# Turned operands stored token by token, and read with a step, in a recurrence and mixing kernel on one core

## The chip, the cores and the metric

The kernel runs on one core of a Trainium2 chip, with fp32 inputs in HBM and an fp32 output there. The metric is the time of one execution on the device in microseconds (us); less is better. The engines are TensorE (PE, with its weight loads shown apart as PEld), VectorE (DVE), ScalarE (ACT), GpSimd (POOL) and SyncE (SP, which only issues transfers here).

## The reference

Four batches, eight heads, 768 tokens, 40 numbers per head. The first part is a recurrence over tokens with a 40x40 state for each head; its output, with the heads side by side (320 numbers per token), goes through a mixing block.

```python
for t in range(S):
    y[:, :, t] = np.einsum('bhd,bhde->bhe', rt, state)
    Sa = np.einsum('bhde,bhe->bhd', state, at)
    state_decay = state * wt[:, :, None, :] - np.einsum('bhd,bhe->bhde', Sa, bt)
    state = state_decay + np.einsum('bhd,bhe->bhde', vt, kt)

theta = x @ w_theta
zr, zi = x * np.cos(theta), x * np.sin(theta)
y = np.einsum('ts,bsd->btd', w_tok_r, zr) + np.einsum('ts,bsd->btd', w_tok_i, zi)
u = x + y
out = u + np.maximum(u @ w_ch, 0.0)
```

## The kernel before

**Chunks.** The recurrence is computed in chunks of 128 tokens: 6 chunks per batch, 24 in all, numbered i. For each chunk, decays are summed by a product with a triangular matrix, k, b and a are scaled by them, and the scaled operands are turned (transposed on TensorE) so that heads and their 40 numbers lie on partitions. Two heads share a turned block: head 2g on partitions 0 to 39, head 2g+1 on 64 to 103. So there are G = 4 pairs g, and a turned operand of a chunk is a tile of 128 partitions x 512 bf16 numbers. Between tokens of the chunk there are four score matrices (`scores`, lines 530 to 553): `spsi` and `sphi` from kbT and aT, `slv` from vT and rT, `slu` from nuT and rT. Each is eight matmuls of 64x128 by 64x128 (4 pairs x 2 halves of the partitions), all at line 537, into a tile of two PSUM banks, and then a masked copy to SBUF. `recurrence` takes the state on by one chunk, `readout` makes the chunk's output: at line 723 four matmuls of rT against the state of before, with rT as the stationary operand, then for each head one with `lamv` (line 730) and one with `lamu` (line 732).

**How r and v are turned.** r is loaded for two chunks at a time in long runs (line 405): partition p of the loaded tile is 4t + g, t counting groups of eight tokens, and eight tokens q lie along the partition. `turn_runs` (line 500) casts this to bf16 and makes eight transposes (line 509), one for each q, into one PSUM bank; within each the 128 columns are (t, g). Two copies on ScalarE (line 513), one for each of the two chunks, read that bank with a step and write SBUF in the order (g, t, q), so that in rT the 128 tokens of a pair g lie side by side. For chunks 0 to 7 (`RUNS = 8`) v is loaded and turned in the same way (tile names `raw_v`, `o`, `vT`), and `turn_back` (line 519) turns vT again into the form with tokens on partitions; for chunks 8 to 23 v is turned from its own cast by `tr` (line 479), pair by pair. That makes 12 calls of `turn_runs` for r and 4 for v: 128 transposes, and 24 + 8 copies at line 513. In all these transposes the tile that is turned is the stationary operand, and the unit matrix `wide` streams.

**Copies of whole words.** Other turned tiles leave PSUM through `evac` (line 386): ScalarE copies pairs of bf16 numbers as 32-bit words (`copy_words`, line 381), or VectorE copies them as bf16 numbers (`copy_halves`, line 384).

**The order of the work.** The program makes a list of operations; each names its engine, and operations may carry an alternative on another engine. `ORDER` gives the order in which the operations are issued, written out by hand as numbers, `HOMES` the PSUM bank of each result, and `PICK` the operations that take their alternative. The costs that an operation is given (592 for the copies at line 513) are not used after that. Before, the copies at line 513 have no alternative, and no number of theirs stands in `PICK`. Waits between engines follow from who writes and reads what.

Of the kernel before, what the change touches and what calls it, by code (L numbers as in the profile page):

```python
# [10 lines left out]
BF16 = mybir.dt.bfloat16  # L11
# [10 lines left out]
RUNS = 8  # L22
# [178 lines left out]
def mm(n):  # L201
    return max(n / 2.4 + 2.5, 25.0)


def tail(n):
    return 166 + n / 2.4 - mm(n)
# [3 lines left out]
def kernel(  # L210
# [14 lines left out]
    nc = tc.nc  # L225
# [4 lines left out]
    G = H // 2  # L230
# [9 lines left out]
    def sb(name, shape, dt, n):  # L240
        return [consts.tile(shape, dt, name=f"{name}_{i}") for i in range(n)]
# [31 lines left out]
    ident = wide[:, 64:192]  # L273
# [46 lines left out]
    for n, (i, t) in sorted(enumerate(to_zero), key=lambda e: e[1][0]):  # L320
# [12 lines left out]
    nuT_t = sb("nuT", [128, 512], BF16, 2)  # L333
# [18 lines left out]
                i=sb("wtok_i", [128, NT, 128], BF16, NT))  # L352
# [7 lines left out]
    def ps(key):  # L360
        h = plan.home[key]
        return doubles[h[0] // 2] if len(h) == 2 else singles[h[0] - DOUBLE]

    def rows(p):
        return slice(64 * p, 64 * p + 64)

    def add(eng, kind, i, fn, cost, reads=(), writes=(), at="tile", **kw):
        return plan.add(eng, kind, i, fn, cost, tuple(reads), tuple(writes),
                        (at, i, kind), **kw)

    def pair(t, g):
        return t[:, 2 * g:2 * g + 2, :].rearrange("p a b -> p (a b)")

    def transpose_pairs(dst, srcs):
        for j, src in enumerate(srcs):
            for g in range(G):
                c = (j * G + g) * 128
                nc.tensor.transpose(out=dst[:, c:c + 128], in_=pair(src, g), identity=ident)  # L378

    def copy_words(out, in_):  # L380
        nc.scalar.copy(out=out.bitcast(FP32), in_=in_)  # L381

    def copy_halves(out, in_):
        nc.vector.tensor_copy(out=out, in_=in_.bitcast(BF16))
# [25 lines left out]
    def run_key(nm, i, c):  # L410
        return ("raw_v", i % 6 + c) if nm == "o" else ("raw_r", i // 2 % 2, c)
# [7 lines left out]
    def cast(kind, i, dst, src, reads, writes, fast):  # L419
        act = ("ACT", lambda: nc.scalar.copy(out=dst, in_=src))  # L420
        pool = ("POOL", lambda: nc.gpsimd.tensor_copy(out=dst, in_=src))
        one, two = (act, pool) if fast else (pool, act)
        add(one[0], kind, i, one[1], 0, reads, writes, alts=(two,))
# [76 lines left out]
    def turn_runs(nm, i, t, raw, dsts):  # L500
        s = i // 2 % 2
        cast(nm, i, t[:, :, :, 0:D], raw.rearrange("p c (q d) -> p q c d", q=8),
             [run_key(nm, i, 0), run_key(nm, i, 1)], [(nm, s)], i == 0)
        pr = ("ps", "t" + nm, i)

        def go():
            d = ps(pr).bitcast(BF16)
            for q in range(8):
                nc.tensor.transpose(out=d[:, q * 128:q * 128 + 128],  # L509
                                    in_=t[:, q].rearrange("p c d -> p (c d)"), identity=ident)  # L510
        add("PE", "t" + nm, i, go, 8 * mm(128), [(nm, s)], [pr], new=(pr, 1), tail=tail(128))
        for x, (dst, dkey) in enumerate(dsts):
            add("ACT", "e" + nm, i + x, lambda x=x, dst=dst: nc.scalar.copy(  # L513
                out=dst.rearrange("p (g t q) -> p g t q", g=G, q=8),
                in_=ps(pr).bitcast(BF16).rearrange(
                    "p (q t g) -> p g t q", q=8, g=G)[:, :, 16 * x:16 * x + 16]),
                592, [pr], [dkey])

    def turn_back(i):
        p, vT, vb = ("ps", "tb", i), vT_t[i % NTR], v_t[i % NRV]  # L520

        def go():
            d = ps(p).bitcast(BF16)
            for g in range(G):
                nc.tensor.transpose(out=d[:, g * 128:g * 128 + 128],
                                    in_=vT[:, g * 128:g * 128 + 128], identity=ident)
        add("PE", "tb", i, go, 4 * mm(128), [("vT", i % NTR)], [p], new=(p, 1), tail=tail(128))
        evac("ACT", "eb", i, p, vb.rearrange("p h d -> p (h d)"), 512, writes=[("v", i % NRV)])

    def scores(i, kind, kindm, lhs, rhs, keys, dst, dkey, mask):  # L530
        p = ("ps", kind, i)

        def go():
            t = ps(p).rearrange("p a (g c) -> p a g c", g=G)
            for g in range(G):
                for q in range(2):
                    nc.tensor.matmul(t[:, q, g, :],  # L537
                                     lhsT=lhs[rows(q), g * 128:(g + 1) * 128],
                                     rhs=rhs[rows(q), g * 128:(g + 1) * 128],
                                     start=True, stop=True)  # L540
        add("PE", kind, i, go, 8 * 26, keys, [p], new=(p, 2), mode=64, tail=tail(128))
        flat = dst.rearrange("p a b c -> p (a b) c")
        sign = -1.0 if mask is mask_n else 1.0

        def whole():
            return ps(p).rearrange("p a (g c) -> p (a g) c", c=128)
        add("DVE", kindm, i, lambda: nc.vector.tensor_tensor(  # L547
            out=flat, in0=whole(), in1=mask.to_broadcast([128, 2 * G, 128]), op=ALU.mult),
            1217, [p], [dkey], alts=(("ACT", lambda: nc.scalar.mul(
                out=flat, in_=whole(), mul=sign)),))  # L550
        add(None, "sel", i, None, 0, [dkey], [dkey], alts=(("POOL", lambda: nc.gpsimd.affine_select(
            out=flat, in_=flat, pattern=[[0, 2 * G], [1, 128]], compare_op=ALU.is_gt,
            fill=0.0, base=0, channel_multiplier=-1)),))

    def attention_scores(i):
        st, s2 = i % NTR, i % NSC
        kbT, aT, vT, rT = kbT_t[st], aT_t[st], vT_t[st], rT_t[i // 2 % 3][:, i % 2]
        scores(i, "spsi", "mpsi", kbT[:, 0:512], aT, [("kbT", st), ("aT", st)],
               psi_t[s2], ("psi", s2), mask_p)
        scores(i, "sphi", "mphi", kbT[:, 512:], aT, [("kbT", st), ("aT", st)],  # L560
               phi_t[s2], ("phi", s2), mask_n)
        scores(i, "slv", "mlv", vT, rT, [("vT", st), ("rT", i % 6)],
               lamv_t[s2], ("lamv", s2), mask_p)

    def recurrence(i):
# [114 lines left out]
    def x_key(q):  # L680
        return ("xs", q % 2) if alone(q) else ("x", q % NX)
# [27 lines left out]
    def readout(i):  # L709
        first = i % NCH == 0  # L710
        s2 = i % NSC
        rT, kb = rT_t[i // 2 % 3][:, i % 2], kb_t[i % NKB]
        scores(i, "slu", "mlu", nuT_t[i % 2], rT,
               [("nuT", i % 2), ("rT", i % 6)], lamu_t[s2], ("lamu", s2), mask_p)
        lamv, lamu = lamv_t[s2], lamu_t[s2]
        gd = gd_t[(i + 1) % 2]
        pk = ("ps", "y", i)

        def y():
            t = ps(pk)  # L720
            for g in range(G):
                if not first:
                    nc.tensor.matmul(t[:, g * 80:g * 80 + 80],
                                     lhsT=rT[:, g * 128:(g + 1) * 128],
                                     rhs=gd[:, 2 * g:2 * g + 2, :], start=True,
                                     stop=False, skip_group_check=True)
                for p in range(2):
                    h = 2 * g + p
                    o = t[:, h * D:h * D + D]
                    nc.tensor.matmul(o, lhsT=lamv[:, p, g, :], rhs=kb[:, 0, h, 0:D],  # L730
                                     start=first, stop=False, skip_group_check=True)
                    nc.tensor.matmul(o, lhsT=lamu[:, p, g, :], rhs=kb[:, 1, h, 0:D],  # L732
                                     start=False, stop=True, skip_group_check=True)
        add("PE", "y", i, y, 16 * 25 + (0 if first else 4 * mm(80)),
            [("rT", i % 6), ("lamv", s2), ("lamu", s2), ("kb", 0, i % NKB),
             ("kb", 1, i % NKB)] + ([] if first else [("gd", (i + 1) % 2)]), [pk],
            new=(pk, 1), tail=tail(40))
        x = x_of(i)
        add("DVE", "ex", i, lambda: nc.vector.tensor_tensor(
            out=x.rearrange("p (g c d) -> p g c d", c=2, g=G),  # L740
            in0=ps(pk)[:, 0:DM].rearrange("p (g c d) -> p g c d", c=2, g=G),
            in1=we_t[i % NEX].rearrange("p (g c d) -> p g c d", c=2, g=G),
            op=ALU.mult), 488, [pk, ("we", i % NEX)], [x_key(i)])
# [186 lines left out]
    for o in plan.order():  # L930
        if o.idx in WARM:
            t = ps(o.new[0])
            t = t[:, 0] if len(t.shape) == 3 else t
# [39 lines left out]
```

## Time and profile before

| | |
|---|---|
| time, median of 3 runs | 201.24 us (200.72 to 202.55) |
| the profiled execution's own time | 199.71 us |
| its span, first to last instruction | 198.0 us |
| TensorE, VectorE, ScalarE, GpSimd busy | 96%, 85%, 79%, 72% of the span |
| transposes of r and v, line 509 | 96 + 32 |
| score matmuls, line 537 | 384 of kbT and aT, 192 of vT and rT, 192 of nuT and rT |
| matmuls with rT as stationary operand, line 723 | 80 |
| copies of rT and vT, line 513 | 24 of 596 ns, 8 of 590 ns |

A row of a group of instructions reads: line, engine, operation, what is written <- what is read, shapes and number of them | busy time in us, mean ns of one | idle time of the engine just ahead of them, with what ended it. Matmuls run in a pipeline: the time of one includes its way through the array, and the next starts long before it ends, so the distance between starts tells what one costs. PEld rows are weight loads, which run beside the matmuls.

### The profile page before, as it was taken

Reading aid. Unit: us, or ns where it says so; the run is one execution under the profiler, and the core shown is the slowest. Engines: PE = TensorE matmul, PEld = TensorE weight load, DVE = VectorE, ACT = ScalarE, POOL = GpSimd, SP = SyncE. Lnnn points to the kernel's source line nnn. Section 1 sums busy time; section 2 is a strip of 40 time slices with the busy share of each in tenths; the row PEclk is TensorE's granted clock in tenths of the full one; section 3 lists DMA queues with packets and bytes.
Section 4 is the critical chain, followed back from the end, with each engine's and each line's share of the span. In section 5 each row is a group of like instructions: output and inputs, shape, how many; then the busy total and the mean of one; then the engine's idle time right before and its main releaser. Section 6 shows DMA issues by size and latency. Waiting matters only on the chain.

```text
span 198.0 us, 8123 instructions
## 1 busy us (share of the span) xinstructions
PE 189.6 (96%) x3354; PEld 153.8 (78%) x3354; DVE 167.6 (85%) x263; ACT 156.2 (79%) x345; POOL 142.3 (72%) x207
## 2 busy tenths in 40 slices
PE   7888999998999999999999999999999999999992
PEld 6777787876887788877787978887788878777761
DVE  5279899999999898986897999999999986878553
ACT  3687889999999989699986898889998957565110
POOL 8277574689998999799799767888598684319300
PEclk9999999999999999999999999999999999999999
DMA  6999899999999899999989989989947350020213
GB/s 117 220 195 200 147 199 188 201 179 201 184 196 174 161 196 181 225 190 209 185 189 167 205 183 205 175 171 174 195 73 160 74 140 3 33 70 15 89 66 132
DMA packets 127365, 31.03 MB, mean 157 GB/s; under 512 B 117664, under 2 KB 127328, under 8 KB 127328
## 3 DMA queue, kind: packets, MB, share of 16 engines
q1 hardware_dynamic: 124544, 27.54, 69.5%
q0 software_dynamic: 2784, 2.97, 9.7%
q8 instruction: 26, 0.43, 0.9%
q14 instruction: 11, 0.09, 0.1%
HBM read 29.54 MB, written 3.93 MB: 169 GB/s over the span
## 4 chain that ended last, share of the span: by engine, by line
PE 71%; ACT 10%; SPq 6%; DVE 5%; issue 4%; DMA 2%; POOL 0%; DVEq 0%; ACTq 0%
PE ps_s L809 16%; PE ps_s L378 12%; PE ps_d L537 9%; PE ps_s L693 6%; SPq L395 4%; PE ps_s L661 4%; PE ps_s L617 3%; PE ps_s L509 3%; DMA raw_kb<-in_k_dram 2%; PE ps_s L703 2%; PE ps_s L596 2%; SPq L407 2%; PE ps_s L732 2%; PE ps_s L884 2%; PE ps_d L809 2%
## 5 line engine op out<-in xcount | busy, mean ns | idle before, releaser
L415 POOL TENSOR_TENSOR kb<-raw_kb,ex 128x320 bf16<-128x320 f32 x46 | 36.9, 812 | 8.1 <-ACT ex L448 2.7
L809 PE MATMUL ps_s<-zr,wtok_r 128*128 128x320 bf16 x132 | 37.5, 299 | 0.0
L809 PE MATMUL ps_s<-zi,wtok_i 128*128 128x320 bf16 x132 | 37.5, 299 | 0.0
L547 DVE TENSOR_TENSOR lamu<-ps_d,mask_p 128x1024 bf16<-128x1024 f32 x23 | 27.9, 1216 | 0.3 <-PE ps_d L537 0.3
L547 DVE TENSOR_TENSOR psi<-ps_d,mask_p 128x1024 bf16<-128x1024 f32 x22 | 26.8, 1218 | 0.7 <-PE ps_d L537 0.5
L547 DVE TENSOR_TENSOR phi<-ps_d,mask_n 128x1024 bf16<-128x1024 f32 x19 | 23.2, 1219 | 1.4 <-PE ps_d L537 1.4
L793 POOL TENSOR_TENSOR zi<-cs,xp 128x320 bf16<-128x320 f32 x21 | 16.4, 793 | 9.2 <-ACT cs L778 9.2
L547 DVE TENSOR_TENSOR lamv<-ps_d,mask_p 128x1024 bf16<-128x1024 f32 x17 | 20.7, 1219 | 2.6 <-PE ps_d L537 2.4
L415 POOL TENSOR_TENSOR ah<-raw_a,we 128x320 bf16<-128x320 f32 x22 | 19.0, 868 | 4.0 <-ACT we L457 3.0
L793 POOL TENSOR_TENSOR zr<-cs,xp 128x320 bf16<-128x320 f32 x21 | 16.6, 804 | 2.2 <-ACT cs L778 2.2
L809 PEld LDWEIGHTS <-wtok_r 128*128 128x128 bf16 x144 | 14.0, 97 | 4.1
L537 PE MATMUL ps_d<-aT,kbT 64*128 64x128 bf16 x384 | 16.9, 217 | 0.3 <-ACT kbT L381 0.2
L632 POOL TENSOR_TENSOR gt<-sum,ex 128x320 bf16<-128x320 f32 x13 | 9.6, 736 | 10.6 <-DVE sum L628 7.6
L809 PEld LDWEIGHTS <-wtok_i 128*128 128x128 bf16 x144 | 14.0, 97 | 3.4
L378 PE MATMUL ps_s<-wide,kb 128*128 128x128 bf16 x192 | 15.3, 223 | 0.5 <-ACT th L758 0.3
L513 ACT COPY rT<-ps_s 128x512 bf16<-128x512 bf16 x24 | 13.3, 596 | 1.9 <-PE ps_s L509 1.6
L730 PE MATMUL ps_s<-kb,lamv 128*128 128x40 bf16 x192 | 14.7, 180 | 0.0
L732 PE MATMUL ps_s<-kb,lamu 128*128 128x40 bf16 x192 | 14.6, 179 | 0.0
L537 PEld LDWEIGHTS <-kbT 64*128 64x128 bf16 x384 | 11.7, 94 | 3.5 <-ACT kbT L381 1.3
L833 DVE SCALAR_TENSOR_TENSOR oo<-ps_s,up 128x320 f32<-128x320 f32 x21 | 9.5, 486 | 5.1 <-PE ps_s L703 4.2
L730 PEld LDWEIGHTS <-lamv 128*128 128x128 bf16 x192 | 13.2, 96 | 0.5
L378 PEld LDWEIGHTS <-kb 128*128 128x128 bf16 x192 | 12.0, 100 | 1.4 <-POOL kb L415 0.6
(166 smaller groups left out, 615.8 us busy)
## 6 DMA issues: line engine op xcount, KB each, us to landing
raw_w<-in_w_dram SPq DMA_DIRECT2D x24, 160.0 KB, 4.0
raw_v<-in_v_dram SPq DMA_DIRECT2D x24, 160.0 KB, 3.9
raw_a<-in_a_dram SPq DMA_DIRECT2D x24, 160.0 KB, 4.0
raw_kb<-in_k_dram SPq DMA_DIRECT2D x24, 160.0 KB, 3.8
raw_kb<-in_b_dram SPq DMA_DIRECT2D x24, 160.0 KB, 4.2
raw_r<-in_r_dram SPq DMA_DIRECT2D x24, 160.0 KB, 3.7
out_dram<-oo SPq DMA_DIRECT2D x23, 160.0 KB, 2.2
wrow_i<-in_moe_w_tok_i_dram POOLq DMA_DIRECT2D x6, 192.0 KB, 5.1
```

The costliest lines, as they stand in the source:

```text
L378: nc.tensor.transpose(out=dst[:, c:c + 128], in_=pair(src, g), identity=ident)
L415: pool = ("POOL", lambda: nc.gpsimd.tensor_tensor(out=dst, in0=in0, in1=in1, op=ALU.mult))
L513: add("ACT", "e" + nm, i + x, lambda x=x, dst=dst: nc.scalar.copy(out=dst.rearrange("p (g t q) -> p g t q", g=G, q=8), in_=ps(pr).bitcast( ...
L537: nc.tensor.matmul(t[:, q, g, :], lhsT=lhs[rows(q), g * 128:(g + 1) * 128], rhs=rhs[rows(q), g * 128:(g + 1) * 128], start=True, stop=True)
L547: add("DVE", kindm, i, lambda: nc.vector.tensor_tensor(out=flat, in0=whole(), in1=mask.to_broadcast([128, 2 * G, 128]), op=ALU.mult), 1217 ...
L632: add("POOL", "wgt", i, lambda: nc.gpsimd.tensor_tensor(out=new_state, in0=sum_t, in1=wm.to_broadcast([128, 8, D]), op=ALU.mult), 830, [(" ...
L693: nc.tensor.matmul(ps(pk)[:, 0:DM], lhsT=lhs[:, c * n + kt, :], rhs=wt[:, 3 * c + kt, :], start=kt == 0, stop=kt == 2, skip_group_check=n ...
L730: nc.tensor.matmul(o, lhsT=lamv[:, p, g, :], rhs=kb[:, 0, h, 0:D], start=first, stop=False, skip_group_check=True)
L732: nc.tensor.matmul(o, lhsT=lamu[:, p, g, :], rhs=kb[:, 1, h, 0:D], start=False, stop=True, skip_group_check=True)
L793: pool = ("POOL", lambda: nc.gpsimd.tensor_tensor(out=dst, in0=in0, in1=in1, op=ALU.mult))
L809: nc.tensor.matmul(acc(), lhsT=wtok[nm][j][:, s], rhs=zs[c][:, s], start=n == 0 and c == 0, stop=n == NT - 1 and c == 1)
L833: add("DVE", "oo", t, lambda ck=ck, u=u, oo=oo: nc.vector.scalar_tensor_tensor(out=oo, in0=ps(ck)[:, 0:DM], scalar=0.0, in1=u, op0=ALU.max ...
```

## The change

The eight transposes of `turn_runs` write to PSUM with a step: for each token (t, q) its four pairs g lie side by side (8 bytes), and the tokens of the two chunks follow one another. The two halves of the bank are then each the wanted tile in the order (token, g), and ScalarE copies each as 256 32-bit words. The copies are given an alternative on VectorE; `ORDER`, `HOMES` and `PICK` stay as they are. Where rT is read (scores `slv` and `slu`, line 723), and vT of chunks 0 to 7 (`slv`, `turn_back`), a pair's 128 tokens now lie four numbers apart; `by_token` gives these views and `by_pair` the ones with neighbouring tokens, which the other operands keep.

```diff
+    def by_pair(t):
+        return [t[:, g * 128:g * 128 + 128] for g in range(G)]
+
+    def by_token(t):
+        return [t.rearrange("p (t g) -> p g t", g=G)[:, g] for g in range(G)]
...
         def go():
-            d = ps(pr).bitcast(BF16)
+            d = ps(pr).bitcast(BF16).rearrange("p (t q g) -> p q t g", q=8, g=G)
             for q in range(8):
-                nc.tensor.transpose(out=d[:, q * 128:q * 128 + 128],
+                nc.tensor.transpose(out=d[:, q],
                                     in_=t[:, q].rearrange("p c d -> p (c d)"), identity=ident)
...
-            add("ACT", "e" + nm, i + x, lambda x=x, dst=dst: nc.scalar.copy(
-                out=dst.rearrange("p (g t q) -> p g t q", g=G, q=8),
-                in_=ps(pr).bitcast(BF16).rearrange(
-                    "p (q t g) -> p g t q", q=8, g=G)[:, :, 16 * x:16 * x + 16]),
-                592, [pr], [dkey])
+            words = ("ACT", lambda x=x, dst=dst: copy_words(
+                dst, ps(pr)[:, 256 * x:256 * x + 256]))
+            halves = ("DVE", lambda x=x, dst=dst: copy_halves(
+                dst, ps(pr)[:, 256 * x:256 * x + 256]))
+            add("ACT", "e" + nm, i + x, words[1], 512, [pr], [dkey], alts=(halves,))
...
     def turn_back(i):
...
                 nc.tensor.transpose(out=d[:, g * 128:g * 128 + 128],
-                                    in_=vT[:, g * 128:g * 128 + 128], identity=ident)
+                                    in_=by_token(vT)[g], identity=ident)
...
     def scores(i, kind, kindm, lhs, rhs, keys, dst, dkey, mask):
...
                     nc.tensor.matmul(t[:, q, g, :],
-                                     lhsT=lhs[rows(q), g * 128:(g + 1) * 128],
-                                     rhs=rhs[rows(q), g * 128:(g + 1) * 128],
+                                     lhsT=lhs[g][rows(q)], rhs=rhs[g][rows(q)],
                                      start=True, stop=True)
...
-        scores(i, "slv", "mlv", vT, rT, [("vT", st), ("rT", i % 6)],
+        scores(i, "slv", "mlv", (by_token if i < RUNS else by_pair)(vT), by_token(rT),
+               [("vT", st), ("rT", i % 6)],
                lamv_t[s2], ("lamv", s2), mask_p)
...
-        scores(i, "slu", "mlu", nuT_t[i % 2], rT,
+        scores(i, "slu", "mlu", by_pair(nuT_t[i % 2]), by_token(rT),
                [("nuT", i % 2), ("rT", i % 6)], lamu_t[s2], ("lamu", s2), mask_p)
...
                     nc.tensor.matmul(t[:, g * 80:g * 80 + 80],
-                                     lhsT=rT[:, g * 128:(g + 1) * 128],
+                                     lhsT=by_token(rT)[g],
                                      rhs=gd[:, 2 * g:2 * g + 2, :], start=True,
                                      stop=False, skip_group_check=True)
```

The calls of `scores` for `spsi` and `sphi` pass `by_pair` of kbT and aT, which is what was read before.

More of the change, by code (lines that the diff above doesn't have):

```diff
@@ L557, in attention_scores @@
         kbT, aT, vT, rT = kbT_t[st], aT_t[st], vT_t[st], rT_t[i // 2 % 3][:, i % 2]
-        scores(i, "spsi", "mpsi", kbT[:, 0:512], aT, [("kbT", st), ("aT", st)],
+        scores(i, "spsi", "mpsi", by_pair(kbT[:, 0:512]), by_pair(aT), [("kbT", st), ("aT", st)],
                psi_t[s2], ("psi", s2), mask_p)
-        scores(i, "sphi", "mphi", kbT[:, 512:], aT, [("kbT", st), ("aT", st)],
+        scores(i, "sphi", "mphi", by_pair(kbT[:, 512:]), by_pair(aT), [("kbT", st), ("aT", st)],
                phi_t[s2], ("phi", s2), mask_n)
-        scores(i, "slv", "mlv", vT, rT, [("vT", st), ("rT", i % 6)],
+        scores(i, "slv", "mlv", (by_token if i < RUNS else by_pair)(vT), by_token(rT),
+               [("vT", st), ("rT", i % 6)],
                lamv_t[s2], ("lamv", s2), mask_p)
```

## The prediction

> **What bounds the kernel now.** I read the page first, then the busy time by stretch, then the chain of waits, then single groups and the timeline of TensorE and ScalarE.
>
> ```profile
> span 198.0 us, 8123 instructions
> PE 189.6 (96%) x3354; PEld 153.8 (78%) x3354; DVE 167.6 (85%) x263; ACT 156.2 (79%) x345; POOL 142.3 (72%) x207
> PE 71%; ACT 10%; SPq 6%; DVE 5%; issue 4%; DMA 2%; POOL 0%; DVEq 0%; ACTq 0%
> ```
>
> TensorE carries 71% of the chain that ended last, ScalarE 10%. Busy time by stretch (busy us and count for PE, weight loads, DVE, ACT, POOL) says where each of them rules:
>
> ```profile
> 40.00:50.00 10.00, 9.19 (x173) 7.21 (x171) 9.89 (x13) 9.88 (x23) 9.75 (x14) 1.00 1.03 193
> 50.00:66.00 16.00, 15.67 (x332) 13.01 (x331) 15.46 (x22) 15.91 (x34) 14.59 (x21) 1.00 1.04 185
> 66.00:176.00 110.00, 109.68 (x2025) 90.28 (x2024) 97.07 (x144) 92.83 (x207) 86.37 (x116) 1.00 0.81 155
> ```
>
> From 66 to 176 us TensorE is idle for 0.32 us in 110: that stretch is as long as TensorE's own work. From 40 to 66 us ScalarE is busy 25.79 of 26 us and VectorE 25.35, while TensorE stands for 1.14. Before 19 us the chain is SP's queue of loads and then one load of k (13.93 to 18.56 us), which the change doesn't touch.
>
> **The change part by part.** *The 32 copies on ScalarE (24 of r, 8 of v).* They now read 256 words, a form that the trace has on the same engine:
>
> ```profile
> L513 ACT COPY rT<-ps_s 128x512 bf16<-128x512 bf16 x24 | 13.3, 596 | 1.9 <-PE ps_s L509 1.6 <-DVE up L815 0.2
> L381 ACT COPY kbT<-ps_s 128x512 f32<-128x512 f32 x16 | 9.4, 586 | 2.1 <-PE ps_s L378 1.6
> L381 ACT COPY vT<-ps_s 128x256 f32<-128x256 f32 x15 | 5.7, 380 | 0.8 <-PE ps_s L378 0.7
> ```
>
> So 596 - 380 = 0.216 us less for each, 32 x 0.216 = 6.9 us of ScalarE in all. The written order and the list of operations moved to another engine are unchanged, so all 32 stay on ScalarE and nothing passes another queue. No instruction is listed as waiting for a copy of line 513; the gain goes to what stands behind it on ScalarE. Copies outside a stretch in which the chain runs through ScalarE give nothing. The chain in order of time passes these:
>
> ```profile
> 29.54 0.51 ACT vT L513
> 30.40 0.58 ACT vT L513
> ...
> 31.93 0.36 PE ps_s L596 x8
> 42.42 0.02 ACT vT L513
> ...
> 42.90 0.59 ACT vT L513
> ...
> 89.92 0.26 ACT rT L513
> 90.29 0.59 ACT rT L513
> ```
>
> Three pairs, 6 x 0.216 = 1.3 us at most. TensorE's longest waits behind them are 0.5 us for nx at 31.9 us (the two copies before it are worth 0.43), 0.3 for nu near 45.5, and 0.3 for th near 92.8, sum 1.1. Where ScalarE stops being late, the next is close: from 21.3 to 27.5 us and from 57.3 to 62.5 the chain is on VectorE, whose busy share from 40 to 66 us is 97%. I take 1.0 us, with 0.4 (the VectorE chain swallows all but one pair) and 3.0 as ends. The 3.0 is ScalarE setting the pace everywhere from 20 to 66 us, where 12 of the copies lie (12 x 0.216 = 2.6), and the pair near 90 us (0.4).
>
> *Writing the transposes to PSUM in runs of four 2-byte elements (8 bytes) with 64 bytes from run to run: 16 x 8 = 128 transposes.* No matmul of the trace writes that way. The nearest row is ScalarE's copy of line 513 itself, which reads this bank with 256 bytes between neighbours at 596 ns, against 586 for 512 neighbouring words: hopping costs 10 ns in 512. That is a read, and at 0.83 ns an element. The other end is half the stream rate, which the trace has for the same instruction in its first 10 us:
>
> ```profile
> 6.92 1.03 PE L509 MATMUL ps_s<-wide,o 128*128 128x128 bf16 x8 [0.36 <-ACT o L420]
> 11.88 0.61 PE L509 MATMUL ps_s<-wide,r 128*128 128x128 bf16 x8
> ```
>
> Eight less the last one's own time (219 ns is the median of line 509, 314 the longest, which is among the early ones) give 0.39/7 = 56 ns and 0.72/7 = 102 ns from one to the next: 46 ns more each, 128 x 0.046 = 5.9 us. Nothing below zero: the number of columns stays 128. I take 0, by the row of line 513.
>
> The Trainium skill (PSUM — Partial Sum Buffer, Specifications) says that PSUM's lines are 8 bytes and that any pattern that isn't contiguous slows matmuls significantly. By it the sum would carry the 5.9 us; the reads of line 513 show no such price, and no row here shows a write.
>
> *Reading rT as the moving operand, one 2-byte element in every 8 bytes: 384 score matmuls (lines 562 and 713), in 192 pairs.* A pair (upper and lower 64 rows) starts together:
>
> ```profile
> 91.60 0.39 PE L537 MATMUL ps_d<-rT,vT 64*128 64x128 bf16 x8
> ```
>
> (0.39 - 0.216)/3 = 58 ns from pair to pair, so a pair streams like one 128-column transpose. At half rate the same 46 ns comes on top: 192 x 0.046 = 8.8 us, of which some 0.8 lies before 20 us, beside the loads: 8.0. The lower end is 0. I take 0: two elements of each 16 bytes are still used, and no row of the trace charges a hop; but none shows it on TensorE's input, so the upper end stays for a rival.
>
> The Trainium skill (SBUF — State Buffer, SBUF: two separate sides) gives SBUF lines of 16 bytes and full rate with at least two hits to a line. A step of 8 bytes has exactly two, so by it these matmuls pay nothing.
>
> *Stepped weight loads.* Line 723 loads rT 80 times between short matmuls, in the most closely packed rows of the trace:
>
> ```profile
> 88.57 0.20 PE L723 MATMUL ps_s<-gd,rT 128*128 128x80 bf16 x1
> 88.60 0.18 PE L730 MATMUL ps_s<-kb,lamv 128*128 128x40 bf16 x1
> 88.63 0.18 PE L732 MATMUL ps_s<-kb,lamu 128*128 128x40 bf16 x1
> ```
>
> Starts are 25 ns apart with a load to each, so a load takes 25 ns or less. The 97 ns of a load's own row is latency: it is the same at both rates of issue. At half rate it takes 50, and 25 of that shows: 80 x 0.025 = 2.0 us. The 64 loads of vT in the first eight chunks are worth at most 32 pairs x 0.046 = 1.5 us, most of it before 50 us, where TensorE waits anyway; the 32 of line 525 are hidden under transposes 56 ns apart. So 0 to 3.5 us. I take 0, with the least confidence of all the terms.
>
> Sum: 198.0 - 1.0 = 197.0 us of span. The profiled execution took 199.71 us, 1.7 more than its span, and the median of three runs is 201.24, 1.5 above it. The same 1.0 off the median gives **200.2**; own range 198.9 to 201.2 (gain 2.3 to 0).
>
> **The rivals.**
> 1. *The stepped moving read runs at half rate* (the other side). Place: lines 562 and 713, through line 537; price 8.0 us, with the weight loads 2.0 more. For it: TensorE has no slack from 66 to 176 us. Against it: two elements to each 16 bytes. 201.2 - 1.0 + 8.0 = 208.2, or 210.2 with the loads. It decides from 1.0/192, about 5 ns a pair: 58 becoming 63 undoes the gain.
> 2. *Only the stepped weight loads are slower*: 200.2 + 2.0 to 3.5, about 202.5. For it: a load must bring 128 columns in 25 ns, while a moving operand has 56 for as many, so a load is the first to run short.
> 3. *The PSUM writes are slower*: 200.2 + 5.9 = 206.1.
> 4. *ScalarE was the pace from 20 to 66 us* and all 3.0 us come back: 198.2. For it: ScalarE's 25.79 of 26 us. Against it: VectorE's 25.35 there.
>
> That the copies don't become shorter I rule out: line 381 does the same copy 15 times at 380 ns. What would be late then is nothing new: a copy that ends sooner only frees its bank sooner.
>
> **How the numbers follow.** Forecast (everything stepped is free) 0.34; rival 1: 0.20; rival 2: 0.21; rival 3: 0.12; rival 4: 0.13. One per cent is 2.0 us, about what a measurement of this kernel can tell from no change. Faster by more: rival 4, 0.13. Within: the forecast and two thirds of rival 2, 0.34 + 0.14 = 0.48. Slower: rivals 1 and 3 and the rest of 2, 0.39. The range reaches from rival 4 to rival 3, with 0.5 below and 1.0 above for the weight loads coming together with it: 197.7 to 207.2. Rival 1 (0.20) is left out. As cases of both signs hold much of the chance, the forecast's own range is given above.
>
> **What would show it.** Copies of line 513 become copies of line 381 with about 380 ns. Score matmuls with rT stay at some 58 ns from pair to pair (8 in 0.39 us), like those with aT; 104 would be rival 1. Starts of line 730 after line 723 stay 35 ns apart; 60 would be rival 2. Eight transposes of r stay at 0.61 us; 0.93 would be rival 3. TensorE's waits for nx near 31.9 us, nu near 45 and th near 92.5 become shorter by 0.2 to 0.4 us each; gone together with many small ones before 66 us would be rival 4. Wrong altogether would be a time outside these: TensorE waiting at new places for VectorE.

## The result, and the profile after

| | before | after |
|---|---|---|
| time, median | 201.01 us (200.72 to 202.55, 4 runs) | 209.24 us (208.91 to 209.90, 4 runs) |
| ratio to before, 95% interval | | 1.042 (1.037 to 1.047) |
| span of the profiled execution | 198.0 us | 207.2 us |

The changed kernel is 4.2% slower. (Ratios, here and below, leave out executions that took over 1.5% longer than the fastest of the same kernel; medians and brackets of times are over all runs.) Lines of the code are eight further down after the change (537 is now 545, 723 is 731, 381 is 389, 509 is 517). The page of after, its first two parts and the head of the chain of waits:

```profile
span 207.2 us, 8123 instructions
PE 199.9 (96%) x3354; PEld 161.8 (78%) x3354; DVE 168.7 (81%) x263; ACT 151.5 (73%) x345; POOL 142.1 (69%) x207
...
PE 89%; ACT 3%; DVE 3%; DMA 2%; issue 1%; SPq 1%; ACTq 0%
PE ps_d L545 18%; PE ps_s L817 17%; PE ps_s L386 14%; PE ps_s L701 7%; PE ps_s L669 4%; PE ps_s L517 4%; PE ps_s L625 3%; PE ps_s L604 3%; PE ps_s L711 3%; PE ps_s L740 2%; PE ps_s L892 2%; PE ps_s L592 2%; PE ps_s L738 2%; PE ps_s L731 2%;
```

TensorE now carries 89% of the chain (71% before), and the score products are its first entry with 18% (9% before, in third place). ScalarE's share fell from 10% to 3%. The busy time by stretch (columns as before) shows no idle time of TensorE at all from 66 to 176 us, while ScalarE went from 15.91 of 16 us to 14.75 between 50 and 66 us:

```profile
50.00:66.00 16.00, 15.73 (x318) 13.20 (x317) 15.40 (x20) 14.75 (x34) 13.65 (x20) 1.00 1.06 190
66.00:176.00 110.00, 110.00 (x1935) 90.61 (x1935) 94.33 (x135) 89.51 (x201) 87.12 (x117) 1.00 0.80 152
```

TensorE's timeline of after has the three operations that the change touches: eight transposes of r, a readout, and the same score block that took 0.39 us before.

```profile
11.72 0.61 PE L517 MATMUL ps_s<-wide,r 128*128 128x128 bf16 x8
...
91.72 0.21 PE L731 MATMUL ps_s<-gd,rT 128*128 128x80 bf16 x1
91.76 0.19 PE L738 MATMUL ps_s<-kb,lamv 128*128 128x40 bf16 x1
91.80 0.18 PE L740 MATMUL ps_s<-kb,lamu 128*128 128x40 bf16 x1
...
95.78 0.62 PE L545 MATMUL ps_d<-rT,vT 64*128 64x128 bf16 x8
```

The transposes are at 0.61 us as before, and over all of them the median from one to the next is 56 ns in both kernels: the stepped writes are free. In the readout the second start comes some 40 ns after the first and the third another 40, as far as rows rounded to 10 ns can say; over all 80 the medians are 36 and 36 ns (35 and 26 before). The eight score matmuls take 0.62 us, with 116 ns from pair to pair at the median (56 before). The rows of the tile rT (minimum, median, maximum in ns) say the same for each instruction: 216 became 291 for the moving read, 96 became 112 for the weight load, and the copies went from 592 to 377. First two rows of before, then those of after:

```profile
L537 PE MATMUL ps_d<-rT,vT x192: 216/216/227, 13.9 to 169.7; 64*128 64x128 bf16 x192
L723 PEld LDWEIGHTS <-rT x80: 95/96/100, 25.6 to 178.4; 128*128 128x128 bf16 x80
```
```profile
L545 PE MATMUL ps_d<-rT,vT x192: 270/291/298, 13.8 to 178.3; 64*128 64x128 bf16 x192
L545 PE MATMUL ps_d<-rT,nuT x192: 270/291/293, 15.4 to 184.5; 64*128 64x128 bf16 x192
L731 PEld LDWEIGHTS <-rT x80: 110/112/115, 26.4 to 187.6; 128*128 128x128 bf16 x80
L731 PE MATMUL ps_s<-gd,rT x80: 196/207/210, 26.4 to 187.7; 128*128 128x80 bf16 x80
L389 ACT COPY rT<-ps_s x24: 353/377/417, 12.9 to 176.3; 128x256 f32<-128x256 f32 x24
```

Since TensorE's instructions are the same 3354 in the same order in both kernels, the span can be divided among them, each with the time from its start to the next start (worked out from the starts in the two traces):

| us on TensorE, start to next start | before | after | difference |
|---|---|---|---|
| 384 score matmuls with rT moving | 14.21 | 24.84 | +10.63 |
| readout (lines 731, 738, 740) | 12.97 | 13.57 | +0.60 |
| transposes at lines 517 and 533 | 10.73 | 10.70 | -0.03 |
| 384 score matmuls with aT moving | 14.19 | 14.09 | -0.10 |
| all others | 141.07 | 139.18 | -1.89 |
| before the first, after the last | 4.84 | 4.83 | -0.01 |
| span | 198.0 | 207.2 | +9.2 |

So 11.2 us were paid for stepped reads and 2.0 came back as shorter waits. The experiments ask three things: whether the reads are the cause and which of them; what decides the price of a stepped read; and what the copies were worth.

### The profile page after: what moved, and what is told of

Its sections match the earlier page's. It is cut to its first block, busy times and chain, and to the rows that moved or that the text cites. A ratio compares the mean times of both kernels' runs of the same rounds, so it can differ in the third digit from the quotient of the medians.

```text
span 207.2 us, 8123 instructions
## 1 busy us (share of the span) xinstructions
PE 199.9 (96%) x3354; PEld 161.8 (78%) x3354; DVE 168.7 (81%) x263; ACT 151.5 (73%) x345; POOL 142.1 (69%) x207
## 4 chain that ended last, share of the span: by engine, by line
PE 89%; ACT 3%; DVE 3%; DMA 2%; issue 1%; SPq 1%; ACTq 0%
PE ps_d L545 18%; PE ps_s L817 17%; PE ps_s L386 14%; PE ps_s L701 7%; PE ps_s L669 4%; PE ps_s L517 4%; PE ps_s L625 3%; PE ps_s L604 3%; PE ps_s L711 3%; PE ps_s L740 2%; PE ps_s L892 2%; PE ps_s L592 2%; PE ps_s L738 2%; PE ps_s L731 2%; PE ps_s L449 2%; PE ps_s L586 2%
## 5 line engine op out<-in xcount | busy, mean ns | idle before, releaser
L801 POOL TENSOR_TENSOR zr<-cs,xp 128x320 bf16<-128x320 f32 x21 | 16.8, 809 | 2.7 <-ACT cs L786 2.7
L545 PE MATMUL ps_d<-rT,nuT 64*128 64x128 bf16 x192 | 14.9, 287 | 0.6 <-DVE psi L554 0.5
L738 PE MATMUL ps_s<-kb,lamv 128*128 128x40 bf16 x192 | 15.4, 183 | 0.0
L740 PE MATMUL ps_s<-kb,lamu 128*128 128x40 bf16 x192 | 15.3, 179 | 0.0
L545 PEld LDWEIGHTS <-kbT 64*128 64x128 bf16 x384 | 12.5, 96 | 3.4 <-ACT kbT L389 1.2
L545 PE MATMUL ps_d<-rT,vT 64*128 64x128 bf16 x192 | 14.6, 289 | 0.2 <-ACT vT L389 0.2
L738 PEld LDWEIGHTS <-lamv 128*128 128x128 bf16 x192 | 13.9, 99 | 0.6 <-issue 0.2
L456 ACT ACTIVATE ex<-ps_s 128x328 f32<-128x328 f32 x24 | 10.7, 449 | 4.2 <-PE ps_s L452 3.6
```

The lines of the kernel that those rows point to most:

```text
L456: got = add("ACT", "exp", i, lambda: nc.scalar.activation(out=ex.rearrange("p h x -> p (h x)"), in_=ps(pk)[:, 0:DM + 8], func=AF.Exp), 440 ...
L545: nc.tensor.matmul(t[:, q, g, :], lhsT=lhs[g][rows(q)], rhs=rhs[g][rows(q)], start=True, stop=True)
L801: pool = ("POOL", lambda: nc.gpsimd.tensor_tensor(out=dst, in0=in0, in1=in1, op=ALU.mult))
```

## The experiments

On the chips of the experiments the kernel of before scattered between 200.0 and 206.3 us and was itself slower in the median (202.5 to 203.5 us on three chips, 201.0 for the result), so differences under one per cent are read from the starts on TensorE, not from the times.

**Without the stepped reads.** All readers take neighbouring numbers; writes and copies stay as changed.

```diff
     def by_token(t):
-        return [t.rearrange("p (t g) -> p g t", g=G)[:, g] for g in range(G)]
+        return [t[:, g * 128:g * 128 + 128] for g in range(G)]
```

> The changed kernel with every stepped read of rT and vT replaced by a read of 128 neighbouring numbers (the products then take other tokens than the reference asks for, the same amount of work). The stepped writes to PSUM and the 256-word copies stay. Theory M (the stepped moving read runs at half rate on TensorE, from 56 to 115 ns a pair in the trace of after): all the loss is gone and only the gain of the copies is left, about 200.0 us against 201.0 before, between 199.0 and 200.6; score matmuls back to 216 ns. Rival O (the shorter copies or the stepped writes upset the written order, so that new waits make the loss): it stays near 209.

Measured: 202.18 us (200.73 to 204.91, 10 runs), 1.0046 of before (0.9997 to 1.0095). The loss is gone, so rival O falls: neither the order nor the writes make it. The gain of the copies did not show, and the time is above the 199.0 to 200.6 that theory M gave. The rows of rT are back at 216 ns with the short copies in place:

```profile
L545 PE MATMUL ps_d<-rT,vT x192: 216/216/227, 14.0 to 172.9; 64*128 64x128 bf16 x192
...
L389 ACT COPY rT<-ps_s x24: 352/378/411, 13.2 to 171.4; 128x256 f32<-128x256 f32 x24
```

The profiled execution (span 201.2 us) has one long stop, in TensorE's timeline and in the list of waits of 70 to 85 us:

```profile
78.11 0.39 PE L386 MATMUL ps_s<-wide,kb 128*128 128x128 bf16 x4
80.50 0.23 PE L386 MATMUL ps_s<-wide,kb 128*128 128x128 bf16 x1 [2.00 <-POOL kb L423]
```
```profile
POOL kb L423 <- DMA raw_kb<-in_b_dram: 1.8, 1, 1.8
```

A load of b came late, GpSimd's product of it too, and TensorE stood for 2.0 us. Before that, between 43 and 64 us, this execution had already fallen 1.2 us further behind that of before: there TensorE waits 1.7 us in all for GpSimd's products and casts (lines 423 and 429), which it doesn't in the kernel before, and GpSimd waits for loads of r and b. No copy stands among these waits; whether the shorter copies change when the loads start isn't shown. The page's DMA row stands at 8 and 9 tenths in nearly every slice from 5 to some 145 us.

**Only the moving operand stepped, and only the loads stepped.** The first keeps `by_token(rT)` in the two calls of `scores` alone:

```diff
-        scores(i, "slv", "mlv", (by_token if i < RUNS else by_pair)(vT), by_token(rT),
+        scores(i, "slv", "mlv", by_pair(vT), by_token(rT),
...
-                                     lhsT=by_token(rT)[g],
+                                     lhsT=by_pair(rT)[g],
...
-                                    in_=by_token(vT)[g], identity=ident)
+                                    in_=by_pair(vT)[g], identity=ident)
```

> The changed kernel with only the score products' moving operand rT stepped; the loads of rT at the state product and of vT read neighbouring numbers (other tokens than asked for, the same amount of work). Theory M: nearly the time of the changed kernel, 208.2 to 209.0, as the loads are worth 0.036 us in each of 20 readouts, 0.7 us in all. Rival L (the stepped weight loads are what costs): near 200.5.

The second has `by_pair(rT)` there and keeps `by_token` elsewhere.

> The changed kernel with only the weight loads stepped (rT at the state product, vT in the scores of chunks 0 to 7 and in turn_back); the moving operand rT of the scores reads neighbouring numbers (other tokens than asked for, the same amount of work). Theory M: the time without stepped reads plus 0.5 to 1.0 us. Rival L: near 208. A load behind short matmuls (25 ns apart) should show about 10 ns each, one behind matmuls of 56 ns nothing.

Measured: 208.90 us (208.58 to 210.06, 4 runs), 1.0395 of before (1.029 to 1.050), with the moving operand stepped; 203.93 (200.46 to 205.04, 4 runs), 1.0156 (0.998 to 1.034), with the loads stepped. The second interval is too wide to tell a loss from none, so the rows decide. First the moving operand alone, then the loads alone:

```profile
L545 PE MATMUL ps_d<-rT,vT x192: 270/291/293, 13.8 to 179.5; 64*128 64x128 bf16 x192
...
L731 PEld LDWEIGHTS <-rT x80: 95/96/100, 26.6 to 188.8; 128*128 128x128 bf16 x80
```
```profile
L545 PE MATMUL ps_d<-rT,vT x192: 216/216/246, 13.7 to 170.3; 64*128 64x128 bf16 x192
...
L731 PEld LDWEIGHTS <-rT x80: 110/112/115, 26.6 to 179.2; 128*128 128x128 bf16 x80
```

Each price stays with its own read. The same division as above gives 24.73 us for the score matmuls and 12.91 for the readout in the first kernel, 14.12 and 13.56 in the second. Rival L falls: stepped loads cost 0.6 us, the stepped moving read 10.6.

**A finer interleave.** Two pairs side by side instead of four: runs of 4 bytes in PSUM, a step of 4 bytes in the reads.

```diff
-            d = ps(pr).bitcast(BF16).rearrange("p (t q g) -> p q t g", q=8, g=G)
+            d = ps(pr).bitcast(BF16).rearrange("p (h t q l) -> p q t h l", h=2, q=8, l=2)
...
-            words = ("ACT", lambda x=x, dst=dst: copy_words(
-                dst, ps(pr)[:, 256 * x:256 * x + 256]))
+            words = ("ACT", lambda x=x, dst=dst: nc.scalar.copy(
+                out=dst.bitcast(FP32).rearrange("p (h n) -> p h n", h=2),
+                in_=ps(pr).rearrange("p (h x n) -> p x h n", h=2, x=2)[:, x]))
...
-        return [t.rearrange("p (t g) -> p g t", g=G)[:, g] for g in range(G)]
+        return [t.rearrange("p (h t l) -> p h l t", h=2, l=2)[:, g // 2, g % 2] for g in range(G)]
```

> The changed kernel with a finer interleave: PSUM holds for each token two pairs of heads side by side (runs of 4 bytes), then the same for the other two pairs; the copies still move 256 words, and rT and vT are read with a step of two numbers (4 bytes) instead of four (8 bytes). Theory M1 (what counts is how many bytes lie between the numbers): at 4 bytes the moving read is at full rate, 56 ns a pair, and the time is about 200.0 us, faster than before. Theory M2 (any step above one number halves the rate): 115 ns a pair and about 209. Between them, with 70 to 90 ns a pair, 203 to 206. The writes in runs of 4 bytes should still be 56 ns from one transpose to the next.

> The interleave of two numbers, in five rounds: by theory M (a moving read costs by the bytes that it passes over, and is free up to 4) it loses nothing against before, and gains the copies' 1.0 us where the loads of that chip leave room for it: 0.990 to 1.003 of before. A ratio above 1.01 would mean a price that the trace of a pair (58 ns against 56) doesn't show.

Measured: 203.28 us (200.48 to 205.24, 10 runs), 1.0011 of before (0.994 to 1.008); then, in a second measurement, 202.47 (200.07 to 206.19, 12 runs), 0.9968 (0.992 to 1.001). The 4% are gone. The rows of rT in the second of these runs:

```profile
L548 PE MATMUL ps_d<-rT,vT x192: 214/216/311, 13.7 to 174.2; 64*128 64x128 bf16 x192
...
L734 PEld LDWEIGHTS <-rT x80: 96/97/100, 26.6 to 182.9; 128*128 128x128 bf16 x80
L734 PE MATMUL ps_s<-gd,rT x80: 196/196/202, 26.6 to 182.9; 128*128 128x80 bf16 x80
...
L522 ACT COPY rT<-ps_s x24: 352/378/418, 12.9 to 172.6; 128x256 f32<-128x256 f32 x24
```

All of the copies' shortening is there, and both reads are at their old times within 2 ns: from pair to pair it is 58 ns at the median (56 before), and the score matmuls with rT take 14.61 us from start to start (14.21 before). Some of that, and the 311, is from one block near 82 us, where the granted clock was 0.50 (82 to 84 us). Theory M2 (any step halves the rate) falls, M1's rate stands. M1's time of about 200.0 us wasn't reached: it is the better form of the change, but no faster than before that these runs can tell.

**The price by itself.** Matmuls were added behind the last one of the kernel of before; nothing reads their results. The cut shows the loops for the moving operand and for the results in PSUM; those for pairs of 64 rows and for the stationary operand are built alike.

```diff
+    def every(t, k):
+        return t[:, 0:128 * k].rearrange("p (t g) -> p g t", g=k)[:, 0]
...
+    for k in (1, 2, 3, 4, 8):
+        for _ in range(12):
+            mm_(one[:, 0:128], busy, every(flat, k))
...
+    for k in (1, 2, 4):
+        for _ in range(12):
+            mm_(every(one, k), busy, flat[:, 0:128])
```

> The kernel of before with a row of matmuls added after its last one, whose results nobody reads: twelve 128x128 matmuls for each step (1, 2, 3, 4, 8 numbers of 2 bytes) of the moving operand, the same in pairs on the upper and lower 64 rows, 24 matmuls of 40 columns for each step of the stationary operand, and twelve whose fp32 results are written with a step of 1, 2, 4 words. Theory M1 (bytes between the numbers): moving at steps 1 and 2 some 56 ns from start to start, at step 4 about 115, at step 8 at least that. Theory M1a (one window of 8 bytes for each two numbers, so that only whole windows count): step 3 about 56 to 86, in between, and step 8 no worse than step 4. Theory M1b (the price grows with the distance): step 8 about 230. Loads behind 40 columns: 25 ns at step 1, some 35 at step 4. Words written with a step: no expectation but 56 if PSUM charges no hop.

Measured in one execution (218.91 us with the added work). TensorE's timeline shows the four rows: moving operand stepped, the same in pairs of 64 rows, stationary operand stepped, results stepped.

```profile
198.77 6.68 PE L950 MATMUL ps_s<-zr,busy 128*128 128x128 bf16 x60
205.39 3.43 PE L950 MATMUL ps_d<-zr,busy 64*128 64x128 bf16 x60
208.75 4.25 PE L950 MATMUL ps_s<-busy,zr 128*128 128x40 bf16 x120
212.85 3.45 PE L950 MATMUL ps_s<-zr,busy 128*128 128x128 bf16 x36
```

Within them, the median distance from start to start (for pairs, from pair to pair), in ns:

| step | 1 | 2 | 3 | 4 | 8 |
|---|---|---|---|---|---|
| moving, 128 rows | 56 | 58 | 87 | 116 | 227 |
| moving, pairs of 64 rows | 56 | 58 | 87 | 116 | 227 |
| stationary, behind 40 columns | 25 | 25 | 27 | 33 | 60 |
| fp32 results in PSUM | 56 | 109 | | 109 | |

From step 2 on the moving read costs about 29 ns for each number of the step (58/2, 87/3, 116/4, 227/8 = 29, 29, 29, 28): it costs as if all the bytes from its first number to its last were read, some 9 bytes per ns and partition (8 x 2 x 128 bytes in 227 ns), and 56 ns is what the 128 columns take anyway. M1b is right, M1a falls. The surprise is the last row: fp32 words written with a step cost nearly double, while the transposes' 8-byte and 4-byte runs cost nothing. It is not the slow stream of the kernel's first 10 us come back: there matmuls start 107 ns apart and a weight load takes 151 ns, here it is 109 and 139, from the first stepped write on.

**What the copies were worth.** First where TensorE sets the pace: the stepped reads with the old copies and writes.

```diff
-            d = ps(pr).bitcast(BF16).rearrange("p (t q g) -> p q t g", q=8, g=G)
+            d = ps(pr).bitcast(BF16).rearrange("p (q n) -> p q n", q=8)
...
-            words = ("ACT", lambda x=x, dst=dst: copy_words(
-                dst, ps(pr)[:, 256 * x:256 * x + 256]))
...
+            add("ACT", "e" + nm, i + x, lambda x=x, dst=dst: nc.scalar.copy(
+                out=dst.rearrange("p (g t q) -> p g t q", g=G, q=8),
+                in_=ps(pr).bitcast(BF16).rearrange(
+                    "p (q t g) -> p g t q", q=8, g=G)[:, :, 16 * x:16 * x + 16]),
+                592, [pr], [dkey])
```

> The writes to PSUM and the copies of 512 numbers as before, with the stepped reads of the change (the products take other tokens than asked for, the same amount of work): the price of the reads alone. By the prediction's own term for the copies (1.0 us) it is 1.0 us over the changed kernel, 209.5 to 211 us. If the copies give nothing also where TensorE is the pace: the same as the changed kernel within 0.4 us, about 209.

> The stepped reads with the old copies of 512 numbers and the old writes (other tokens than asked for, the same amount of work), beside the changed kernel on the same chip. If the copies are worth 1.0 us where TensorE is the pace: 0.5 to 1.5 us over the changed kernel. If nothing: within 0.3 us of it.

> The changed kernel itself, beside the next one on the same chip: 208.6 to 210.0. By theory M its score products with rT take 24.8 us of TensorE from start to start (14.2 before), whatever the chip.

Measured: 209.87 us (209.59 to 210.12, 4 runs) on one chip; on another 210.20 (209.46 to 210.21, 4 runs), beside 209.32 (209.06 to 209.62, 4 runs) for the changed kernel, which on that chip is 1.035 of before (1.029 to 1.040) and takes 24.85 us for its score matmuls with rT, as in the result. The old copies are 0.9 us slower, but the two traces of that chip put most of the difference before 24 us. Of the difference at TensorE's last start (1.14 us), 0.82 is already there at the 300th start, near 24 us; there the list of waits of 13 to 24 us of the kernel with old copies has this line:

```profile
POOL ah L423 <- DMA raw_a<-in_a_dram: 1.4, 1, 1.4
```

The changed kernel's list hasn't got it: this load of a landed at 18.8 us, in the changed kernel at 16.8. From there to the end the old copies lose 0.3 us. Whether the other runs' 0.9 is made up in the same way isn't known.

Then two kernels with fewer loads (a and w are not loaded from chunk 5 on): that of before, and the one without stepped reads. The first differs from the kernel of before by this alone, the second from the kernel without stepped reads:

```diff
             add("SP", "l" + key[0][4:], i,
+                None if i >= 5 and key[0] in ("raw_a", "raw_w") else
                 lambda dst=dst, src=src: nc.sync.dma_start(out=dst, in_=src),
```

> The kernel of before without the loads of a and w from chunk 5 on (later chunks work on the numbers left in the buffers), so that less than three quarters of the bytes are loaded. Theory D (up to 90 us the loads keep the DMA engines full, and what ScalarE gains is lost in waiting for them): this kernel loses its waits for loads, 196 to 200 us, and scatters less from run to run than before. Rival N (loads are no limit after 19 us): 200 to 201, as before.

> The kernel without stepped reads (256-word copies, stepped writes, products on neighbouring numbers, which are other tokens than asked for) and without the loads of a and w from chunk 5 on. Theory D: 0.5 to 2 us less than the light kernel of before, as the shorter copies now show. Rival N (the copies are never late, VectorE takes over at once): the same as the light kernel of before within 0.4 us.

Measured: 201.20 us (200.65 to 202.64, 10 runs), 0.992 of before (0.988 to 0.996), and 199.83 (199.26 to 200.27, 4 runs), 0.985 (0.978 to 0.993). Theory D is half right: with fewer loads the shorter copies show, 1.4 us by the medians, and no run of the one kernel overlaps with one of the other. But the light kernel of before didn't go below 200 us, and it scatters little less: 2.0 us over its ten runs, 2.8 over the nine of before on this chip that the ratio uses (201.27 to 204.08).

Nor is all of the 1.4 us the copies'. Of the 1.4 us between the two traces 0.9 is there at the 300th start, near 24 us, and it opens between 10 and 15 us, where the two executions didn't have the same granted clock. The clock rows of their pages, the light kernel of before first (40 slices of 5 us, in tenths of full speed):

```profile
PEclk9969999999999999999999999999999999999999
PEclk9999999999999999999999999999999999999999
```

From 12 to 14 us it was 0.50 against 1.00, while the loads of these microseconds landed no more than 0.2 us later than in the other kernel. Four of the ten runs of the light kernel of before had a mean granted clock of 0.998 or more; their median is 201.1 us, still 1.3 above the other kernel's, so how much of that is the copies' stays open. From the 300th start to the last the shorter copies gain 0.5 us in the traces, at two of the places that the prediction named: TensorE's idle time ahead of nx near 32 us goes from 0.27 us to none, and that ahead of th near 93 us from 0.29 to 0.10.

**Only v token by token.** r is written, copied and read as before, so no moving operand is stepped. The cut shows r's copies; its writes and its readers are put back too.

```diff
         for x, (dst, dkey) in enumerate(dsts):
+            if nm == "r":
+                add("ACT", "e" + nm, i + x, lambda x=x, dst=dst: nc.scalar.copy(
+                    out=dst.rearrange("p (g t q) -> p g t q", g=G, q=8),
...
+                continue
```

> Only v of chunks 0 to 7 is stored token by token and copied as 256 words; r is written, copied and read as before. No moving operand is stepped, only 64 + 32 loads of vT. By theory M no loss, and 8 shorter copies, all before 50 us: 0.995 to 1.003 of before. If stepped loads did cost (rival L): above 1.005.

Measured: 202.40 us (199.83 to 206.52, 12 runs), 0.9978 of before (0.993 to 1.003): no change that can be told, so the 96 stepped loads of vT cost nothing that shows.

## Why the prediction was wrong

- *The step that failed* is "Reading rT as the moving operand, one 2-byte element in every 8 bytes ... I take 0". Its reasons were that "two elements of each 16 bytes are still used" and that no row of the trace charged a hop. The only row of a hop was ScalarE's copy, and it was the wrong neighbour: it shows another engine reading PSUM, at some 0.8 ns a number by the prediction's own rows ((586 - 380)/256), and TensorE takes 0.44 (56 ns for 128). The read costs 116 instead of 56 ns a pair, 10.6 us in all. The runs with only the moving read stepped and with no stepped read show that it makes nearly all of the loss. This is rival 1, which had a chance of 0.20 and was the one left out of the range. That its times of 208.2 and 210.2 lie so near the measured 209.24 is partly luck: its 8.0 us for the reads was 2.6 too small, and the waits shrank by 2.0 us instead of 1.0.
- *Its upper end* of 8.0 us was too small as well. It took the half rate of the first 10 us (102 ns) for the worst case. That was a slower stream of all matmuls at the start of the kernel, not a stepped read: in the probe the price goes by the bytes passed over, and 8 of them cost 116. Each block also ends later: from its last start to the next instruction it is 223 ns at the median instead of 148 (some 113 instead of 53 where the next is another block with rT). And the 0.8 us taken off for what lies before 20 us was too much: three of the 48 blocks lie there, 0.55 us at 46 ns a pair.
- The Trainium skill (SBUF — State Buffer, SBUF: two separate sides) has full rate with at least two hits to a line of 16 bytes. For this read the runs disagree: step 4 has two hits and takes 116 ns, step 2 has four and takes 58. The measurement decides.
- *The stepped weight loads*, taken at 0 with 3.5 us as the upper end, cost 0.6 us: some 8 ns on each of 80 (33 against 25 in the probe), not the 25 that a halved rate would give. Rival 2's mechanism is there, at 0.6 us where 2.0 to 3.5 were named. The sign written down for it looked one instruction too early: from line 723 to line 730 it is 36 ns instead of 35, and the delay stands between 730 and 732, 36 instead of 26.
- *The stepped writes*, taken at 0, are free: 0.61 us for eight, as written down for that case. Rival 3 falls. The Trainium skill's sentence on PSUM (PSUM — Partial Sum Buffer, Specifications) agrees with the fp32 results of the probe, 109 instead of 56 ns, and not with these runs of bf16 transposes.
- *The copies* became as short as forecast (383 and 375 ns, forecast 380). What that was worth isn't settled. The times say 0.9 us with stepped reads and 1.4 with fewer loads and none; the traces show 0.3 and 0.5 behind the 300th start, about the lower end of 0.4, and the rest arises before it, where one trace has a later load and the other a lower granted clock. The forecast of 1.0 is neither borne out nor refuted. Of its three waits that for nu near 45 us didn't shorten at all: 0.30 us before, after and in both light kernels. That for nx was misread: at 31.9 us it is 0.27, and the 0.5 is another one, at 13.2 us. Rival 4's 3.0 us came back in no run.
- *What was late next* was named as VectorE. In the profiled execution of the kernel without stepped reads it was a load. That the DMA engines stand at 8 to 9 tenths from 5 to some 140 us was on the page of before and was not used.
- *TensorE without slack from 66 to 176 us* was right and is why the price came through almost whole: 11.2 us paid, 2.0 us of waits saved. The copies' part of the 2.0 is the open size above; the rest are waits whose releasers had more time; which of them came first wasn't taken apart.

## What to carry to other kernels

Before a layout is changed to make a copy cheap, count what reads the result and on which engine: 32 copies gained 0.2 us each on an engine with little say in the time, and 384 matmuls paid 28 ns each on the one that sets it. A row of another engine was no bound for TensorE's operand here; where no row shows a stepped operand, the upper end stays in the range. If an interleave is wanted, keep the step of a bf16 moving operand at two numbers: that gave the same short copies for 2 ns in 58 on TensorE.

## What was not expected of the hardware

- The moving operand's price is proportional to its step from two bf16 numbers on: 58, 87, 116, 227 ns for 128 columns at steps 2, 3, 4, 8.
- The stationary operand suffers far less: behind 40-column matmuls 25, 25, 27, 33, 60 ns at steps 1, 2, 3, 4, 8, so at step 4 it costs 8 ns where the moving one costs 60.
- fp32 matmul results written to every second or every fourth word take 109 ns for 128 columns, both the same; bf16 transposes written in runs of 4 or 8 bytes take 56, as in one piece.
